# Turning w3 by DMA transposes, splitting the first turns and reordering the first loads in a fused attention and feed-forward kernel

## The chip, the cores and the metric

The kernel runs on one core of a Trainium2 chip. The metric is the device time of one execution in microseconds (us), the median of three runs. Engines are named as in the profile: PE is TensorE (its matrix multiplies), PEld its weight loads, DVE is VectorE, ACT is ScalarE, POOL is GpSimd and SP is SyncE. DMAs that POOL issues go by a software queue, which here also rounds float32 to bf16 on the way; those that SP issues go by a hardware queue.

## The reference, cut to what matters

Eight batches of eight heads, 576 positions, 64 features a head. Heads 0 to 3 attend to the last 32 positions; heads 4 to 7 to every fourth of the last 128. Heads are joined and go through a multiplicative feed-forward block with no nonlinearity behind the product, so that `w3 @ w_out` can be formed once and used in place of two products.

```python
scores = (1/8) * q @ k.T                       # per batch and head
rel = pos[:, None] - pos[None, :]
mask_plain = (rel >= 0) & (rel < 32)            # heads 0..3
mask_dil = (rel >= 0) & (rel < 128) & (rel % 4 == 0)   # heads 4..7
attn = softmax(where(mask, scores, -1e9)) @ v
x = attn.transpose(0, 2, 1, 3).reshape(4608, 512)
h = (x @ w1) * (x @ w2) @ w3                    # w1, w2: 512 x 1024; w3: 1024 x 1024
out = h @ w_out                                 # w_out: 1024 x 512
```

## The kernel before, in words

All products run on PE in bf16 with float32 sums in PSUM, which is one tile `ps` of eight banks. The work is cut into tasks. Python code adds each task to a `Plan` with a name, an engine, a duration in ns that is written in the code, the tasks that it depends on, a priority and the number of PSUM banks that it needs. `Plan.run` (lines 70 to 156) walks through time with these durations and gives the order of the tasks and the banks of each; the instructions are then issued in that order, and each engine works through its own part of it strictly in order. So a guess of the planner that is too short makes an engine stand at a wait with later work queued behind it. Loads are tasks of a queue called "DMA": POOL issues them one after the other, and it waits before each for the landing of the load eight places earlier.

What the tasks do:

- `Lqn`, `Lkn`, `Lvn` load q, k and v of one batch (lines 220 to 225), `LW` loads one half of the columns of w1 or w2, `LWO` half of w_out, `LW3.f` rows 128f to 128f+127 of w3. The first q and k (heads 0 to 3 of batch 0) come as float32 by SP into `gt` and are rounded by ACT (`Cqn`, `Ckn`, lines 229 to 240).
- `T...` are DVE block transposes of q, k and v into `qt`, `kt` and `vt` (lines 337 to 357). Heads 0 to 3 are called u = 0, heads 4 to 7 u = 1; for u = 1, and for q of u = 0 too, the four residues of the position modulo 4 are stored one after the other, 144 positions each. `VT` and `VK` bring v of the batches 0 and 1 back by PE transposes (line 366) and copies.
- `S` are scores of a group of blocks of 96 queries (line 408). In the batches 0 and 1 the mask comes as a bias that PE adds first (line 391), from a small table that POOL (`band`) and ACT (`blocks`, lines 308 to 319) make at the start. `E` is the exponential on ACT, `V` the product with v (line 444), `R` and `N` the division on DVE, `X` and `K` the turn back by PE (line 484) and a copy. From batch 2 on a DMA transpose on SP (`XD`, line 497) does the turn back.
- `A` and `B` are the products with w1 and w2 for one of 16 units k of 288 tokens and one of eight column blocks f (line 516, four matmuls each); ACT copies A (`CA`) and DVE multiplies (`G`, line 532).
- `W3T`, `W3C`, `W3M`, `W3D` form `w3 @ w_out`: per row block f of w3, eight PE transposes (line 573) into a PSUM bank, a copy to SBUF by ACT (line 580), eight matmuls (line 585) and a copy to `wf_sb` by DVE (line 595).
- `Y` is the product with `wf_sb` for 128 tokens (line 543); it needs all eight blocks of `wf_sb`. ACT copies it (line 554) and SP stores it.

The order of the first loads is: batch 0, w1 and w2 (two halves each), w_out (two halves), six blocks of w3, batch 1, the last two blocks of w3, then batch 2. The order of A and B is unit by unit, f from 0 to 7. Before unit 0, PE runs `WARM` = 12 matmuls on zeros.

Of the kernel before, what the change touches and what calls it, by code (L numbers as in the profile page):

```python
# [29 lines left out]
BIASED = 2  # L30
TURNED = 2
ORDER = (2, 3, 0, 1)
RANK = dict(E=1.5, VK=1, K=0.4, N=3, T=1.5, VT=0.2, S=0.3, V=0.1, X=0.4)
WARM = 12
W3_FIRST = 6
SHIFT = {}
ON_DVE = ("K0.0", "K0.2", "K0.3", "K1.2", "VK0.1.0", "VK1.0.1")
GRP = 5
WHOLE = ("qn", "kn")
TURN_LAT = 2700  # L40
LEAD = 1.4

# [12 lines left out]
class Plan:  # L55
# [14 lines left out]
    def run(self):  # L70
# [41 lines left out]
        while len(order) < n:  # L112
            progress = True
            while progress:
                progress = False
                for e in engines:
                    if free[e] > now:
                        continue
                    for r, t in sorted(waiting[e], key=lambda x: x[1].prio):
                        if r > now:  # L120
                            continue
                        at = place(t) if t.slot else 0
                        if at is not None:
                            break
                    else:
                        continue
                    waiting[e].remove((r, t))
                    t.start = now
                    if e == "DMA":
                        free[e] = now + t.dur[0]  # L130
                        dma = max(dma, now + t.dur[0]) + t.dur[1]
                        t.end = dma + 1900
                    else:
                        t.end = free[e] = now + t.dur
                        if t.lat == TURN_LAT and dma > now:
                            t.lat += 3300
                    if t.slot:
                        t.place = at
                        held[at : at + t.slot] = [t] * t.slot
                        if t.slot == 4:  # L140
                            kept = None
                    order.append(t)
                    for u in users[id(t)]:
                        left[id(u)] -= 1
                        if not left[id(u)]:
                            r = max(d.end + (0 if d.eng == u.eng else d.lat) for d in u.deps)
                            waiting[u.eng].append((r, u))
                    progress = True
# [11 lines left out]
def kernel(  # L160
# [27 lines left out]
    wk_pool = ctx.enter_context(tc.tile_pool(name="wk", bufs=2))  # L188
    w3_pool = ctx.enter_context(tc.tile_pool(name="w3", bufs=8))
    ps_pool = ctx.enter_context(tc.tile_pool(name="ps", bufs=1, space=bass.MemoryType.PSUM))  # L190
# [62 lines left out]
    def load_v_dil(b, m):  # L253
        vp = vps[b % 2]
        r, mu = 2 * (m // 3), m % 3
        runs = {
            0: [(0, 96, r, 0)],
            1: [(0, 48, r, 96), (48, 48, r + 1, 0)],
            2: [(0, 96, r + 1, 48)],
        }[mu]  # L260
# [9 lines left out]

    def load_w(dst, src, c):
        f = slice(512 * c, 512 * (c + 1))
        nc.gpsimd.dma_start(
# [34 lines left out]
    def blocks():  # L308
# [3 lines left out]
        base = bias[:, 6, :]  # L312
        by_res = base.rearrange("p (t r) -> p r t", r=4)
        nc.scalar.copy(
            out=bias[:, 0:4, :].rearrange("p i (r t) -> p i r t", r=4),
            in_=by_res.unsqueeze(1).to_broadcast([P, 4, 4, 24]),
        )
        nc.scalar.copy(out=bias[:, 4, :], in_=base)
# [18 lines left out]
    def turn(b, u, nm, part):  # L337

        src = qk[(nm, b)][:, u, :].bitcast(U32)
        dst, pad = {"qn": (qts, 0), "kn": (kts, PADK), "vn": (vts, PADK)}[nm]  # L340
        d = dst[b % len(dst)].rearrange("p u w c -> p u (w c)").bitcast(U32)[:, u, :]
        if part is None:
            o = d[:, pad : pad + S].rearrange("p (j a) -> p a j", a=18)
            nc.vector.transpose(out=o, in_=src.rearrange("p (a i) -> p a i", a=18))  # L344
            return
        n, first, odd = ((5, 0, 2 * RUN + 4), (4, 2 * RUN, 5 - 2 * RUN))[part]
        o = bass.AP(
            tensor=d.tensor,
            offset=d.offset + pad + first,
            ap=[d.ap[0], [1, n], [RUN, 2], [9, 16], [odd, 2]],  # L350
        )
        i = bass.AP(
            tensor=src.tensor,
            offset=src.offset + part * 64,
            ap=[src.ap[0], [128, n], [32, 2], [1, 32]],
        )
# [200 lines left out]
    def store(i):  # L557
# [3 lines left out]
        while at < end:  # L561
            n = min(end, (at // RUN + 1) * RUN) - at
            b, x = at // S, at % S
            row = b * S + 4 * (x % RUN) + x // RUN
            nc.sync.dma_start(
# [3 lines left out]

    def w3_back(ft):  # L570
        x = bank(KFF * P, BF16).rearrange("p (g x) -> p g x", g=KFF)
        for g in range(KFF):
            nc.tensor.transpose(  # L573
                out=x[:, g, :], in_=w3n[ft][:, g * P : (g + 1) * P], identity=ident
            )
        held[("x3", ft)] = x

    def w3_keep(ft):
        w3T[ft] = wk_pool.tile([P, KFF, P], BF16, tag="w3T", bufs=2, name="w3T")
        nc.scalar.copy(out=w3T[ft], in_=held[("x3", ft)])  # L580

# [11 lines left out]

    def w3_done(ft):
        nc.vector.tensor_copy(out=wf_sb[:, ft, :], in_=held[("wf", ft)])

# [45 lines left out]
    def loads_v(b):  # L642
# [5 lines left out]
        ]  # L648

    def loads_w12(c):  # L650
        return [
            load("LW", 800, 3300, [], lambda d=d, s=s: load_w(d, s, c))
            for d, s in ((w1_sb, moe_w1), (w2_sb, moe_w2))
        ]
# [7 lines left out]
    for u in range(2):  # L662
        for nm in ("qn", "kn", "vn"):
            if u or nm not in WHOLE:
                loads_rows(nm, 0, (u,))
    idt = add("ident", "DMA", (600, 0), [], lambda: make_identity(nc, ident), 2.5, lat=-1900)
    bnd = add("band", "DMA", (700, 0), [c0], band, 2.6, lat=-1800)
    blk = add("blocks", "ACT", 1200, [bnd], blocks, 0, lat=100)
    blk = add("no halo", "DVE", 150, [blk], no_halo, 0, lat=80)
    mk = add("masks", "DMA", (2500, 0), [blk], masks_of_bias, 26.5, lat=-1800)  # L670
    lw12 = [loads_w12(0), loads_w12(1)]
    for c in range(2):
        lwo[c] = load(f"LWO{c}", 600, 3300, [], lambda c=c: load_wo(c))
    def loads_w3(fts):
        for ft in fts:
            lw3[ft] = load(f"LW3.{ft}", 550, 1400, [], lambda ft=ft: load_w3(ft))

    loads_w3(range(W3_FIRST))
    for nm in ("qn", "kn", "vn"):
        loads_rows(nm, 1)  # L680
    loads_w3(range(W3_FIRST, KFF))

    FUSED, w3m = [], []
    for ft in range(KFF):
        x = add(f"W3T{ft}", "PE", 510, [lw3[ft], idt], lambda f=ft: w3_back(f), 6, slot=1,
                after=[w3m[-2] if len(w3m) > 1 else None])
        y = add("W3C", "ACT", 1012, [x], lambda f=ft: w3_keep(f), -1, lat=100,
                after=[w3m[-2] if len(w3m) > 1 else None])
        z = add(f"W3M{ft}", "PE", 1728, [y, lwo[0], lwo[1]], lambda f=ft: w3_mul(f), 7, slot=1)
        w3m.append(z)  # L690
        FUSED.append(add("W3D", "DVE", 688, [z], lambda f=ft: w3_done(f), -1, lat=100))

# [4 lines left out]
    def turns(b, u, nm, pr):  # L697
        parts = (None,) if u == 0 and nm != "qn" else (0, 1)
        old = last_v.get((b - 1, u)) if nm == "vn" else last_s.get((b - 2, u))
        ts = [  # L700
            add(f"T{nm}{b}.{u}.{part or 0}", "DVE",
                1245 if part is None else 750 if part == 0 else 630, [L[(nm, b, u)], c0],
                lambda part=part: turn(b, u, nm, part), pr, lat=80, after=[old])
            for part in parts
        ]
        turned.setdefault((nm, b), []).extend(ts)
        return ts

    vals, T = {}, {}
    for b in range(B):  # L710
# [4 lines left out]
        for u in range(2):  # L715
            T[(b, u)] = [
                t for nm in ("kn", "qn") for t in turns(b, u, nm, 10 * b + RANK["T"])
            ]
        for u in range(2):
            if b >= 2:  # L720
                break
            tv = turns(b, u, "vn", 10 * b + RANK["T"])
            for half in range(2):
                x = add(f"VT{b}.{u}.{half}", "PE", 420, tv + [idt],
                        lambda b=b, u=u, h=half: v_back(b, u, h), b - 99 + RANK["VT"], slot=1)
# [6 lines left out]
                ]  # L732
        if b >= 2:
            hal = add(f"HALO{b}", "DVE", 820, LV[b], lambda b=b: halo_v(b), 10 * b + 2, lat=80)
            for u in range(2):
# [4 lines left out]
        def group(blocks, biased):  # L740
# [3 lines left out]
            n = f"{b}.{2 * u + m // 3}.{m % 3}"  # L744
            need = [t for at in sorted({x[0:2] for x in blocks}) for t in T[at]]
            old = readers.pop(n_grp - len(ets), [])
# [69 lines left out]
    def ups(k, f):  # L816
        nonlocal seq
        b, hf = k // 2, k % 2
        need = kept[b][0:2] + kept[b][2 + hf : 3 + hf]
        wl = lw12[f // 4]  # L820
        lap = k * UNIT - RING
# [25 lines left out]
    done = 0  # L847
    for k in range(2 * B):
        for f in range(KFF):
            ups(k, f)  # L850
            if f % 3 == 1 and done < n_y and (done + 1) * P <= k * UNIT:
                downs(done)
                done += 1
    while done < n_y:
# [43 lines left out]
```

## Time and profile before

| | |
|---|---|
| median of three runs | 259.79 us (259.71 to 260.15) |
| the profiled execution | 260.15 us |
| its span, first to last instruction | 258.4 us |
| mean granted PE clock | 0.985 |
| busy: PE / DVE / ACT / POOL | 246.9 / 166.2 / 122.9 / 65.0 us |
| w3's transposes on PE (line 573) | 64 instructions |
| w3's copies on ACT (line 580) | 8 of 1012 ns |

The profiled execution is one of the three, the longest: its time is 1.75 us more than its span, and 0.36 us more than the median. In the profile, a busy time is the time in which an engine had an instruction in it; matmuls overlap, so that the time that one of them adds to a stream is less than its own duration. The chain of waits, which is followed back from the last instruction, shows what each one adds. A DMA's time runs from its issue to its landing.

### The profile page before, as it was taken

The page shows a single profiled execution, that of the slowest core. Times are in us where ns is not written, and L with a number is a line of the kernel's source. Part 1 is how long each engine was busy: PE and PEld are TensorE (multiplying, and loading weights), DVE is VectorE, ACT ScalarE, POOL GpSimd, SP SyncE. Part 2 cuts the span into 40 slices and gives each one's busy share as a digit, 9 for nine tenths or more (in the row PEclk, how much of TensorE's full clock was granted, in tenths as well). Part 3 has the DMA queues.
Part 4 walks back from the last instruction along what each step waited for, and adds up shares of the span by engine and source line. Part 5 has one row for each costly group of instructions (what it writes and reads, how often), then busy time and mean ns, then how long its engine had stood idle before and what let it go on. Part 6 is the DMA issues. An engine that isn't in the chain of part 4 may idle for free.

```text
span 258.4 us, 6741 instructions
## 1 busy us (share of the span) xinstructions
PE 246.9 (96%) x2732; PEld 168.1 (65%) x2732; DVE 166.2 (64%) x338; ACT 122.9 (48%) x211; POOL 65.0 (25%) x101
## 2 busy tenths in 40 slices
PE   6589999999999999999999999999999999999993
PEld 2367865576577676676667766677766766777661
DVE  3966436979898898898858687666654653333220
ACT  4465464493826373453653535636355343333331
POOL 8612476265401728232023050300000000000000
PEclk9689999999999999999999999999999999999999
DMA  7999999999999999999983949652417172211113
GB/s 224 204 206 200 210 213 210 201 90 193 153 177 159 182 186 128 163 184 213 213 89 49 106 56 143 101 75 55 91 39 93 41 91 63 83 39 43 43 41 122
DMA packets 58030, 33.40 MB, mean 129 GB/s; under 512 B 44688, under 2 KB 47760, under 8 KB 58000
## 3 DMA queue, kind: packets, MB, share of 16 engines
q0 software_dynamic: 37488, 18.81, 57.4%
q1 hardware_dynamic: 20512, 14.16, 26.8%
q8 instruction: 21, 0.34, 0.6%
q14 instruction: 9, 0.07, 0.1%
HBM read 38.80 MB, written 9.44 MB: 187 GB/s over the span
## 4 chain that ended last, share of the span: by engine, by line
PE 92%; ACT 2%; DVE 2%; DMA 2%; issue 0%; ACTq 0%; DVEq 0%
PE ps L516 49%; PE ps L543 24%; PE ps L585 5%; PE ps L444 5%; PE ps L408 4%; ACT et L419 2%; PE ps L391 2%; DMA gt<-in_q_dram 2%; PE ps L366 1%; PE ps L573 1%; PE ps L484 1%; DVE qt L357 1%; DVE kt L344 0%; ACT qn L240 0%; DVE vt L344 0%
## 5 line engine op out<-in xcount | busy, mean ns | idle before, releaser
L516 PE MATMUL ps<-XT,w_sb 128*128 128x288 bf16 x1024 | 136.0, 286 | 0.2 <-DVE gt L532 0.2
L516 PEld LDWEIGHTS <-w_sb 128*128 128x128 bf16 x1024 | 97.6, 98 | 30.2 <-issue 0.6
L532 DVE TENSOR_TENSOR gt<-ps,asb 128x288 bf16<-128x288 f32 x128 | 57.9, 454 | 55.2 <-PE ps L516 53.5
L527 ACT CAST asb<-ps 128x288 bf16<-128x288 f32 x128 | 50.9, 398 | 60.5 <-PE ps L516 57.7
L543 PE MATMUL ps<-wf_sb,gt 128*128 128x512 bf16 x288 | 67.7, 379 | 0.0
L554 ACT COPY osb<-ps 128x512 f32<-128x512 f32 x36 | 21.1, 585 | 52.5 <-PE ps L543 52.5
L543 PEld LDWEIGHTS <-gt 128*128 128x128 bf16 x288 | 28.0, 98 | 27.7
L262 POOL DMA_DIRECT2D vp<-in_v_dram x48 | 30.0, 631 | 49.2 <-PE ps L444 16.2
L419 ACT ACTIVATE et<-ps 128x1920 bf16<-128x1920 f32 (+2 forms) x23 | 34.4, 1506 | 5.9 <-PE ps L408 4.7
L467 DVE TENSOR_TENSOR xo<-ps,rcp 96x384 bf16<-96x384 f32 (+1 forms) x48 | 31.8, 678 | 0.6
L357 DVE STREAM_TRANSPOSE qt<-qn 128x320 uint32<-128x320 uint32 (+1 forms) x32 | 21.6, 675 | 3.3 <-ACT qn L240 3.1
L427 DVE TENSOR_TENSOR et<-et,mask 128x960 bf16<-128x960 bf16 (+1 forms) x30 | 18.1, 630 | 3.8 <-ACT et L419 3.6
L444 PEld LDWEIGHTS <-et 128*128 128x128 bf16 x384 | 14.5, 98 | 3.8 <-ACT et L419 1.3
L444 PE MATMUL ps<-vp,et 128*128 128x65 bf16 x384 | 15.6, 195 | 1.0 <-ACT et L419 1.0
L585 PE MATMUL ps<-wo_sb,w3T 128*128 128x512 bf16 x64 | 15.0, 379 | 0.0
L408 PEld LDWEIGHTS <-kt 32*128 32x128 bf16 x768 | 9.5, 95 | 6.1 <-issue 5.6
L357 DVE STREAM_TRANSPOSE kt<-kn 128x320 uint32<-128x320 uint32 (+1 forms) x16 | 10.9, 681 | 3.6 <-PE ps L408 3.5
L408 PE MATMUL ps<-qt,kt 32*128 32x96 bf16 x768 | 12.9, 206 | 0.0
L344 DVE STREAM_TRANSPOSE kt<-kn 128x576 uint32<-128x576 uint32 x8 | 10.0, 1249 | 2.0 <-PE ps L408 2.0
L580 ACT COPY w3T<-ps 128x1024 bf16<-128x1024 bf16 x8 | 8.1, 1012 | 4.8 <-PE ps L573 4.7
L455 DVE RECIPROCAL rcp<-ps 96x12 f32<-96x12 f32 x32 | 6.5, 214 | 5.6 <-PE ps L444 5.5
L248 POOL DMA_DIRECT2D vp<-in_v_dram x6 | 7.3, 1209 | 10.6 <-PE ps L444 10.6
(49 smaller groups left out, 105.4 us busy)
## 6 DMA issues: line engine op xcount, KB each, us to landing
qn<-in_q_dram POOLq DMA_DIRECT2D x7, 576.0 KB, 8.0
kn<-in_k_dram POOLq DMA_DIRECT2D x7, 576.0 KB, 9.0
w_sb<-in_moe_w_dram POOLq DMA_DIRECT2D x4, 512.0 KB, 12.3
w3n<-in_moe_w_dram POOLq DMA_DIRECT2D x8, 256.0 KB, 15.2
out_dram<-osb SPq DMA_DIRECT2D x8, 256.0 KB, 2.8
out_dram<-osb SPq DMA_DIRECT2D x8, 224.0 KB, 2.8
vp<-in_v_dram POOLq DMA_DIRECT2D x6, 288.0 KB, 10.3
out_dram<-osb SPq DMA_DIRECT2D x8, 192.0 KB, 2.6
```

What stands on the lines that cost most here:

```text
L262: nc.gpsimd.dma_start(out=vp[32 + p0 : 32 + p0 + n, 4:8, m, 0:D], in_=v_rows(b, 4, 4 * t0 + res, [[4 * D, n], [S * D, 4], [1, D]]),)
L357: nc.vector.transpose(out=o, in_=i)
L408: nc.tensor.matmul(out=self.sp[:, g, QB * i : QB * i + QB], lhsT=kt[prt, u, QB * m : QB * m + P, c], rhs=qq, start=(c == 0 and not biased) ...
L419: nc.scalar.activation(out=ev, in_=self.sp[:, :, 0:x], func=ACT.Exp, scale=scale)
L444: nc.tensor.matmul(out=self.o[:, g, mm, :], lhsT=grp.et[:, c0 : c0 + P], rhs=vps[self.b % 2][:, 4 * self.u + g, 3 * self.hf + mm, 0 : D + ...
L467: nc.vector.tensor_tensor(out=dst, in0=self.o[0:QB, hs, :, 0:D], in1=self.rcp[0:QB, hs, :].unsqueeze(3).to_broadcast([QB, n, 3, D]), op=AL ...
L516: nc.tensor.matmul(out=o, lhsT=w_sb[:, c, f * P : (f + 1) * P], rhs=unit_cols(k, c), start=(j == 0), stop=(j == DCH - 1),)
L527: nc.scalar.copy(out=a_sb, in_=held[("a", k, f)])
L532: nc.vector.tensor_tensor(out=gt[:, f, c0 : c0 + UNIT].rearrange("p (r m t) -> p m r t", r=2, m=BLK), in0=held[("b", k, f)].rearrange("p ( ...
L543: nc.tensor.matmul(out=y, lhsT=gt[:, f, c0 : c0 + P], rhs=wf_sb[:, f, :], start=(f == 0), stop=(f == KFF - 1),)
L554: nc.scalar.copy(out=o_sb, in_=held[("y", i)])
L585: nc.tensor.matmul(out=o, lhsT=w3T[ft][:, g, :], rhs=wo_sb[:, g, :], start=(g == 0), stop=(g == KFF - 1),)
```

## The change

Five things change, and the planner lays out all tasks anew.

1. w3 is turned by DMA transposes. `W3T` and `W3C` go; a task `XW` on SP (`w3_turn`) reads one block `w3n` of 128 x 1024 bf16 in SBUF and writes it turned to `w3T`. There are three buffers of `w3T` in place of two, so that XW of block f waits for the matmuls `W3M` of block f-3; and seven of `w3n` in place of eight, so that the load of block 7 waits for XW of block 0. Of the copies `W3D`, five go from DVE to ACT.
2. In batch 0 the turns of q, k and v of heads 4 to 7 are cut into two halves by residue. The residues are stored in the order 0, 2, 1, 3, so that the even tokens can be turned, and their scores begun, first.
3. The first loads come in another order: w1 and w2 in pieces of 256, 256 and 512 columns with block 0 of w3 between them, then batch 1, block 1 of w3, w_out, and blocks 2 to 7 of w3, of which block 7 comes in the midst of batch 2's loads.
4. The units 0 and 1 are interleaved: f = 0 to 3 of both, then f = 4 to 7 of both.
5. `blocks` gets a priority that puts it ahead of `Cqn` and `Ckn` on ACT; its widest copy becomes two; `WARM` is 16; other priorities, the list of copies that go to DVE, and the planner's durations of DMAs are new.

```diff
-RANK = dict(E=1.5, VK=1, K=0.4, N=3, T=1.5, VT=0.2, S=0.3, V=0.1, X=0.4)
-WARM = 12
-W3_FIRST = 6
+RES = (0, 2, 1, 3)
+RANK = dict(E=2, VK=2, K=1.5, N=0.3, T=0.5, VT=0.4, S=0.1, V=0.2, X=0.4)
+WARM = 16
+FIRST_LOADS = ("w0", "30", "w1", "w2", "q1", "k1", "v1", "31", "o0", "o1", "32", "33", "34", "35", "36", "37")
...
-ON_DVE = ("K0.0", "K0.2", "K0.3", "K1.2", "VK0.1.0", "VK1.0.1")
+ON_DVE = ("K0.1", "K0.2", "K0.3", "K1.2", "VK1.0.0", "VK1.1.0", "VK1.1.1", "W3D2", "W3D3", "W3D4")
...
+BUSY_LAT = 3300
...
-                        if t.lat == TURN_LAT and dma > now:
-                            t.lat += 3300
+                        if e == "SP" and t.lat >= TURN_LAT and t.name[0] == "X" and dma > now:
+                            t.lat += BUSY_LAT
+                            dma += t.lat / 6
...
-    w3_pool = ctx.enter_context(tc.tile_pool(name="w3", bufs=8))
+    w3_pool = ctx.enter_context(tc.tile_pool(name="w3", bufs=7))
...
-        n, first, odd = ((5, 0, 2 * RUN + 4), (4, 2 * RUN, 5 - 2 * RUN))[part]
+        n, first, odd = ((5, 0, RUN + 4), (4, RUN, 5 - RUN))[part % 2]
+        low = max(0, part // 2 - 1)
+        both = 2 if part < 2 else 1
...
-    def w3_back(ft):
-        x = bank(KFF * P, BF16).rearrange("p (g x) -> p g x", g=KFF)
-        for g in range(KFF):
-            nc.tensor.transpose(
-                out=x[:, g, :], in_=w3n[ft][:, g * P : (g + 1) * P], identity=ident
-            )
-        held[("x3", ft)] = x
-
-    def w3_keep(ft):
-        w3T[ft] = wk_pool.tile([P, KFF, P], BF16, tag="w3T", bufs=2, name="w3T")
-        nc.scalar.copy(out=w3T[ft], in_=held[("x3", ft)])
+    def w3_turn(ft):
+        w3T[ft] = wk_pool.tile([P, KFF, P], BF16, tag="w3T", bufs=3, name="w3T")
+        nc.sync.dma_start_transpose(out=w3T[ft], in_=w3n[ft])
...
-    blk = add("blocks", "ACT", 1200, [bnd], blocks, 0, lat=100)
+    blk = add("blocks", "ACT", 1200, [bnd], blocks, -5, lat=100)
...
+    WC = (slice(0, 256), slice(256, 512), slice(512, 1024))
...
-    for ft in range(KFF):
-        x = add(f"W3T{ft}", "PE", 510, [lw3[ft], idt], lambda f=ft: w3_back(f), 6, slot=1,
-                after=[w3m[-2] if len(w3m) > 1 else None])
-        y = add("W3C", "ACT", 1012, [x], lambda f=ft: w3_keep(f), -1, lat=100,
-                after=[w3m[-2] if len(w3m) > 1 else None])
-        z = add(f"W3M{ft}", "PE", 1728, [y, lwo[0], lwo[1]], lambda f=ft: w3_mul(f), 7, slot=1)
+    for ft in sorted(lw3):
+        x = add(f"XW{ft}", "SP", 100, [lw3[ft]], lambda f=ft: w3_turn(f), -1, lat=3600,
+                after=[w3m[-3] if len(w3m) > 2 else None])
+        if ft + 7 in lw3:
+            lw3[ft + 7].after.append(x)
+            lw3[ft + 7].deps.append(x)
+        z = add(f"W3M{ft}", "PE", 1728, [x, lwo[0], lwo[1]], lambda f=ft: w3_mul(f), 7, slot=1)
...
-            parts = (None,) if u == 0 and nm != "qn" else (0, 1)
+            parts = (2, 3, 4, 5) if b == 0 else (0, 1)
...
+    half = KFF // 2
+    begin = [(k, f + h) for h in (0, half) for k in range(2) for f in range(half)]
+    for k, f in begin + [(k, f) for k in range(2, 2 * B) for f in range(KFF)]:
```

In the new order on PE, the matmuls of blocks 0 and 1 of w3 stand after the first `V` of batch 1, those of the blocks 2, 3 and 4 one after the other in the midst of unit 2, block 5 after the first scores of batch 2, block 6 after the next ones, and block 7 in unit 3. On SP, the eight XW stand right behind the two first loads and ahead of all other transposes and stores.

## The prediction

> **What bounds the kernel now.** I read the page first: who is busy, when, and who makes the chain that ended last.
>
> ```profile
> PE 246.9 (96%) x2732; PEld 168.1 (65%) x2732; DVE 166.2 (64%) x338; ACT 122.9 (48%) x211; POOL 65.0 (25%) x101
> ...
> PE   6589999999999999999999999999999999999993
> ...
> DMA  7999999999999999999983949652417172211113
> ...
> PE 92%; ACT 2%; DVE 2%; DMA 2%; issue 0%; ACTq 0%; DVEq 0%
> ```
>
> PE is the bound from the fourth slice on (a slice is 6.46 us): whatever leaves PE there shortens the run, if nothing else is late. The DMA row has nines over the first 19 slices, some 120 us: the loads run without a pause. Next the chain in order of time, where w3 is made into w3 @ w_out:
>
> ```profile
> 33.84 0.45 PE ps L573 x8
> 34.29 0.98 PE ps L516 x8
> 35.27 0.45 PE ps L573 x8
> 35.72 1.73 PE ps L585 x8
> ```
>
> PE goes from one task to the next with no gap; eight transposes of w3 (L573) add 0.45 us, eight matmuls with w_out (L585) 1.73, four of L516 0.49. PE's own waits:
>
> ```profile
> PE ps L366 <- DVE vt L344: 4.0, 1, 4.0
> PE ps L604 <- DVE warm L607: 1.2, 1, 1.2
> PE ps L444 <- ACT et L419: 1.0, 2, 0.8
> ```
>
> Past the 4.0 us ahead of v's first turn PE waits some 2 us in all. The start, by windows (PE busy first, the clock third from the end):
>
> ```profile
> 8.00:10.00 2.00, 0.34 (x4) 0.34 (x5) 2.00 (x3) 0.00 (x0) 1.45 (x2) 0.54 1.10 207
> 10.00:12.00 2.00, 2.00 (x15) 1.37 (x13) 1.97 (x6) 1.48 (x2) 0.54 (x2) 0.50 1.15 199
> ...
> 16.00:18.00 2.00, 1.24 (x43) 0.82 (x41) 1.97 (x4) 1.76 (x2) 0.53 (x1) 1.00 1.25 211
> ```
>
> The clock is at half from about 8.2 to 15 us. Last, issue to landing: the loads of w3 (L288), then the transposes of attention's output (L497) while loads run (73 to 119 us), then without loads (from 150 us):
>
> ```profile
> DMA to landing us min/median/max: 12.5/15.2/18.3
> ```
>
> ```profile
> DMA to landing us min/median/max: 5.2/7.5/8.3
> ```
>
> ```profile
> DMA to landing us min/median/max: 2.6/3.4/5.2
> ```
>
> The transposes that the change adds run beside the loads, so the middle row prices them.
>
> **The sum** starts from the profiled execution, 260.15 us (span 258.4); it lies 0.36 above the median of 259.79, which I take off at the end. The tail after PE's last matmul is untouched.
>
> **PE transposes of w3 go.** 8 times 0.45 us, all on the chain: -3.6. ACT loses eight copies of 1012 ns and gets five of 585, DVE loses five of 692; between 34 and 48 us both are busy about half the time, so that counts nothing.
>
> **The start: +0.5.** Before, ACT rounded q from 4.73 and k from 6.08 (1.15 us each), and `blocks` came after. Now `blocks` stands ahead of both and waits for POOL's band, which ends at 4.49. Its copies took 0.54 + 0.27 + 0.23; with the widest in two pieces of some 0.36, 1.2. So q is rounded from 5.8, k until 8.1; DVE turns q (1.41) until 8.4, k (1.24) until 9.6. The first scores start at 9.65, where PE stood at v's turn (9.66) before. From there, at half clock: two groups of scores, 1.56 and 1.67, v's turns 1.46, until 14.3; exponentials (1.13) and v copies (0.80) in ACT's new order end at 16.85 (third exponential), 17.65 and 19.0. On DVE eight half turns (about 0.5 of 0.73 and 0.62 each) last until 15, then the divisions of 0.95 and the copies; the one that unit 0 needs ends at 21.7. Before, unit 0 began at 21.2. Bounds: at full clock the two groups and the turns save 2.2, ACT's chain then ends 1.3 earlier, so -0.8; with every half turn at the whole one's price, +1.0. Four more warm-up matmuls at 0.22 lie in the 4.0 us wait and cost nothing; without that cover 0.9.
>
> The last warm-up matmul ended at 5.69 and the clock fell at about 8.2, 2.5 us later; now it ends near 6.6, and the scores at 9.65 come 3.0 us later, so I take the low clock. The Trainium skill (TensorE: Matmul & The Clock Gate, "What's actually happening") lets the clock fall only after an idle window of some 3.4 us: by that rule it would stay up, and the time would be about 1.3 us less.
>
> **The waits for turned blocks: +1.2.** When does PE need them? Unit 0 from 21.7; 32 tasks of 0.49 and one X of 0.26 bring it to 37.7; the scores and turns of batch 1 took 5.85 (48.84 to 54.69); three V and short waits, 1.5. Block 0 at 45.1 to 46.8, block 1 at 47.1 to 48.8. Then two X, a V, six tasks of 0.49, an X, and 0.5 of waits, 4.6: block 2 at 53.4, 3 at 55.1, 4 at 56.8 to 58.6. Six tasks, scores of 0.55, a task: block 5 at 62.6; 6 at 64.9.
>
> When do they come? The landings move with the order. The first rows end at 11.7; w1 and w2 take 10.7, a w3 block 1.25, batch 1's q, k, v 8.8, w_out 5.3. Block 1 lands at 33.6 and block 2 at 40 to 41. A transpose takes 7.5 us by the row beside loads, but a block of w3 has 262 KB where attention's has 147, 1.78 times. Three of attention's landed 0.6 us apart when the loads had ended (81.3, 81.9, 82.4) and 2.4 apart beside them (109.1, 111.3, 113.9): +0.5 or +1.9. I take 8.2, nearer the first, since most of the 7.5 is waiting and not transfer. Bounds: 3.4 (no load beside it) and 13.4 (all of 7.5 grows by 1.78). Blocks 1 and 2 come at 42 and 49, in time. Then three buffers bind: block 3's transpose starts when block 0's matmuls end, 46.8, and lands at 55.0 (needed 55.1); block 4's at 57.0 (56.8); block 5's at 63.3; block 6's at 65. With each wait moving what follows: 0.2 + 0.5 = 0.7. If instead one must be through before the next (4.3 apart, 1.78 times 2.4), block 4 waits 2.5 and block 6 0.5: 3.0. The three at 109 to 114 had 8.2 each and did not add up, so nearer the first: 1.2. By the outer bounds: 0, or 10.4 (5.1 at block 3, 0.3, 0.5, 4.5).
>
> Who stands behind: on PE everything; on DVE the copies of blocks 2 to 4 are ahead of the turns of batch 2, whose scores come after block 5 anyway; on SP only the next transposes (the first XD is issued past 70 us); on POOL the last loads of batch 2 stand behind block 7's load, which waits for block 0's transpose, issued at 16, and so for nothing.
>
> **The rest: +0.3.** Batch 1's scores and the begin of unit 2 wait for ACT and DVE some 0.3 more than the 0.7 before, since less PE work is interleaved with them. The order of f, the residues' order and the loads' pieces leave counts and durations as they are: 0 (w's pieces of 256 columns are ready at 18, needed from 21.7; that cover gone, 1.3 each).
>
> Sum: -3.6 + 0.5 + 1.2 + 0.3 = -1.6; 260.15 - 1.6 - 0.36 = **258.2**. Own range: waits of 0 and a start of -0.8 give 255.7, waits of 2.2 give 259.2.
>
> **Rival 1, slower: transposes land in the order of issue.** The POOL row "14.55 ... [2.01 <-DMA w_sb" says that eight loads are always queued, 12 to 18 us deep. All ten transposes from 73 to 119 us landed between 1.2 before and 1.5 after the last load issued ahead of them (100.8 to 109.06: the load ahead landed at 109.77). If that holds at depth, with 1.4 us of DMA time each: block 1 (issued at 35.0 behind seven loads) lands at 48.0, block 2 behind q and k of batch 2 at 55.1, block 3 behind v at 58.9, block 6 behind batch 3 at 70.9. Waits: 0.9, 0.7, 2.1, 0.1, 2.2: 6.0. The time is 260.15 - 3.6 + 0.5 + 0.3 + 6.0 - 0.36 = **263.0**. It decides from waits of 2.8, a latency near 9.5 us. Against it: none of the ten had more than 9.1 us of loads ahead.
>
> The Trainium skill (DMA: Bandwidth & Descriptors, "Queues, rings and completion order") says that a DMA engine takes the queues that have work in turn, a packet of one at a time. By that rule a transpose waits for one load's packet and not for seven loads, and the forecast stands; by the landings above alone it would be the rival.
>
> **Rival 2: no change.** The transposes come in time, but each adds its packets to a full DMA, eight times 1.0 to 1.4 us, and batch 2 and the transposes of blocks 4 to 6 slip: waits near 2.8, within 0.5 of 259.8.
>
> **How the numbers follow.** Forecast 0.50, rival 1 0.33, rival 2 0.17, of which I give 0.10 to a change within 0.2% (0.5 us, about what a measurement of this kernel can tell from none) and 0.07 to slower. So faster 0.50, same 0.10, slower 0.40. The range, 255.9 to 263.4, takes in the own range but for its foot, rival 2, and rival 1 with 0.4 to spare; outside it lie rival 1 with still longer waits (up to the 10.4 above, 267.4) and little else.
>
> **What would show it.** In the profile after: no PE transposes of w3; transposes `w3T<-w3n` on SP with 7 to 9 us to landing (right), 12 or more (rival 1); PE's waits at the matmuls with w_out near 1 us or near 6; the clock still at half until about 15 us and unit 0 at 21.7. A first XD or store held up, or scores of batch 2 waiting for q, would make the sum wrong in a way not foreseen.

## The result, and the profile after

The changed kernel takes 277.31 us (four runs, 274.29 to 278.63) where the kernel before took 259.97 beside it. The ratio is 1.063, with a 95% interval of 1.054 to 1.071. It is slower by 6%, and the forecast of 258.2 us was wrong, as was its range. The profiled execution of the changed kernel took 274.29 us, with a span of 272.5 us. (The kernels in which DMA turns w3 scatter by up to 4% from one execution to the next, and a few executions of the others are longer too; a ratio is made from undisturbed executions alone.)

The page of the changed kernel, the lines that answer to those shown of before:

```profile
PE 247.4 (91%) x2672; PEld 165.2 (61%) x2672; DVE 164.7 (60%) x340; ACT 115.7 (42%) x208; POOL 66.2 (24%) x103
...
PE   8679896099599997999999999999999999999993
...
PEclk9999999569979999999999999999999999999998
DMA  7999999999999499979989953972232232212113
...
PE 70%; DMA 24%; POOL 2%; ACT 1%; issue 1%; DVE 0%; SPq 0%; DVEq 0%; POOLq 0%; ACTq 0%
```

PE is no busier than before (247.4 to 246.9 us: 3.6 us of transposes went, and work at half clock came), but it has holes: the eighth slice (47.7 to 54.5 us) is a zero. In and behind the holes its clock is down. DMA is 24% of the chain where it was 2%. PE's waits, in total us, number and longest:

```profile
PE ps L587 <- DMA w3T<-w3n: 12.2, 3, 8.6
PE ps L418 <- DVE kt L352: 2.1, 1, 2.1
PE ps L454 <- DVE vp L276: 1.4, 1, 1.4
```

L587 are the matmuls with w_out, and they wait for turned blocks: 12.2 us where the sum had 1.2. The chain from 36 to 79 us (start, us, what):

```profile
36.67 17.15 DMA w3T<-w3n
...
53.87 3.60 PE ps L587 x8
...
64.09 11.20 DMA w3T<-w3n
...
75.34 3.14 PE ps L587 x8
```

Block 1's transpose took 17.15 us from issue to landing, and PE stood for 8.60 of them; block 5's took 11.20, and PE stood for 3.19. The packet records divide block 1's time: 3.8 us from the issue to its first packet, 12.3 for its 1024 packets of 256 bytes (40.48 to 52.74 us), 1.1 from the last one to the landing. The transposes go through their queue one after another: block 2 was issued at 43.46, but its first packet follows block 1's last, at 52.76. Eight matmuls that take 1.73 us at full clock take 3.60 and 3.14 right after. The line of the transposes in the code (L582), issue to landing:

```profile
DMA to landing us min/median/max: 8.6/11.4/17.1
```

By stretches (us, PE busy first, the granted clock third from the end):

```profile
6.00:8.00 2.00, 0.75 (x6) 0.29 (x3) 1.70 (x3) 1.39 (x2) 1.84 (x4) 1.00 1.09 200
8.00:10.00 2.00, 1.14 (x44) 0.79 (x48) 2.00 (x3) 0.65 (x1) 1.29 (x2) 1.00 1.10 207
...
43.00:54.00 11.00, 2.40 (x25) 1.30 (x22) 3.62 (x7) 1.13 (x2) 6.60 (x9) 0.75 1.13 190
54.00:59.00 5.00, 5.00 (x33) 2.74 (x32) 0.46 (x1) 1.13 (x2) 1.15 (x2) 0.52 1.59 145
```

At the start the clock stays at full speed, against the forecast. PE's order of time there (start, us, what, and the wait ahead of it):

```profile
6.10 0.65 PE L401 MATMUL ps<-bias,ident 128*128 128x288 bf16 x4
8.86 0.44 PE L418 MATMUL ps<-qt,kt 32*128 32x96 bf16 x24 [2.10 <-DVE kt L352]
```

The bias matmuls of the first group need only the mask blocks, which are ready early now; they run right behind the warm-up, and PE then stands 2.1 us and not 3. Unit 0 begins at 18.83 us where it began at 21.17.

So the span grew by 14.1 us in this way: turns -3.6, start -2.3, waits for turned blocks +12.2, and PE's work at half clock +4.2 (4.9 us of it from 53.87 to 58.77 and 3.4 from 75.84 to 79.25, half of which is extra). Some 3.6 remain, 2.2 of which are new waits for gt (0.8) and v (1.4); the last 1.4 were not taken apart.

### The profile page after: what moved, and what is told of

It is laid out like the page before. It is cut to its first block, busy times and chain, and to the rows that moved or that the text cites. A ratio compares the mean times of both kernels' runs of the same rounds, so it can differ in the third digit from the quotient of the medians.

```text
span 272.5 us, 6621 instructions
## 1 busy us (share of the span) xinstructions
PE 247.4 (91%) x2672; PEld 165.2 (61%) x2672; DVE 164.7 (60%) x340; ACT 115.7 (42%) x208; POOL 66.2 (24%) x103
## 4 chain that ended last, share of the span: by engine, by line
PE 70%; DMA 24%; POOL 2%; ACT 1%; issue 1%; DVE 0%; SPq 0%; DVEq 0%; POOLq 0%; ACTq 0%
PE ps L526 39%; PE ps L553 20%; DMA w3n<-in_moe_w_dram 11%; DMA w3T<-w3n 10%; PE ps L587 4%; PE ps L454 3%; DMA out_dram<-osb 3%; PE ps L418 3%; ACT et L429 1%; ACT osb L564 1%; POOL w_sb L279 1%; PE ps L494 0%; POOL vn L232 0%; DVE vp L276 0%; POOL qn L232 0%
## 5 line engine op out<-in xcount | busy, mean ns | idle before, releaser
L269 POOL DMA_DIRECT2D vp<-in_v_dram x48 | 29.8, 626 | 57.5 <-PE ps L454 21.2
L587 PE MATMUL ps<-wo_sb,w3T 128*128 128x512 bf16 x64 | 17.9, 434 | 12.2 <-DMA w3T<-w3n 12.2
L367 DVE STREAM_TRANSPOSE qt<-qn 128x320 uint32<-128x320 uint32 (+3 forms) x34 | 22.5, 665 | 2.8 <-DMA qn<-in_q_dram 1.6
L587 PEld LDWEIGHTS <-w3T 128*128 128x128 bf16 x64 | 6.4, 106 | 20.8 <-DMA w3T<-w3n 13.1
L367 DVE STREAM_TRANSPOSE kt<-kn 128x320 uint32<-128x320 uint32 (+3 forms) x18 | 11.6, 645 | 0.6 <-PE ps L418 0.4
L598 ACT CAST wf_sb<-ps 128x512 bf16<-128x512 f32 x5 | 2.9, 585 | 21.0 <-PE ps L587 20.9
L232 POOL DMA_DIRECT2D kn<-in_k_dram x8 | 5.5, 690 | 21.3 <-DVE kt L367 18.8
```

The costliest lines, as they stand in the source:

```text
L269: nc.gpsimd.dma_start(out=vp[32 + p0 : 32 + p0 + n, 4:8, m, 0:D], in_=v_rows(b, 4, 4 * t0 + res, [[4 * D, n], [S * D, 4], [1, D]]),)
L367: nc.vector.transpose(out=o, in_=i)
L587: nc.tensor.matmul(out=o, lhsT=w3T[ft][:, g, :], rhs=wo_sb[:, g, :], start=(g == 0), stop=(g == KFF - 1),)
```

## The experiments

Theory A is the prediction's rival 1: a transpose lands after the loads that were issued ahead of it, so that the depth of the queue makes it late. Theory B: the DMA engines take one packet of the transpose and one of a load in turn, so that each of its 1024 packets waits for a load's packet, whatever stands behind that. Theory C: it is other parts of the change that cost.

**All but the turns (e1).** The task `XW` is taken out, and PE's transposes and ACT's copy are put back; the planner lays the tasks out anew.

```diff
-        x = add(f"XW{ft}", "SP", 100, [lw3[ft]], lambda f=ft: w3_turn(f), -1, lat=3600, ...
+        t = add(f"W3T{ft}", "PE", 510, [lw3[ft], idt], lambda f=ft: w3_back(f), 6, slot=1, ...
+        x = add("W3C", "ACT", 1012, [t], lambda f=ft: w3_keep(f), -1, lat=100, ...
```

> Everything of the change but one part: w3 is turned on PE and copied by ACT again, as in the kernel before. If the turned blocks are what costs (theories A and B alike, whatever makes them late), the 12.2 us of waits at the matmuls with w_out and the some 4.4 us of PE work at half clock that follow them go, the eight PE turns (3.6 us) come back, and the earlier start (unit 0 at 18.8 instead of 21.2 us) stays: 255.5 to 258.5 us, below the kernel before. If other parts cost (theory C: the load order, the halves of batch 0, the rounding), it stays above 262 us.

Measured: 257.11 us (median of 257.09 to 268.71; ratio to before 0.988, 0.986 to 0.990). Unit 0 begins at 18.88 us, the clock is full until the last 1.3 us, and the chain reads

```profile
PE 88%; DVE 5%; ACT 3%; issue 2%; POOL 1%; POOLq 0%; DVEq 0%; ACTq 0%
```

Theory C falls. The DMA turns, with the order that the planner makes for them, account for the 20.2 us between the medians of the two kernels, and the rest of the change is worth 3.2 us (before took 260.31 beside it).

**The turns alone, in the old order (e4).** The kernel before, with `XW` in place of `W3T` and `W3C`, three buffers of w3T and seven of w3n.

> The kernel before with one part of the change alone: w3 turned by DMA transposes (three buffers), in the old load order, where the blocks of w3 land at 29 to 35 us ahead of batch 1 and are needed early. Theory A (order of issue): the transposes are issued right behind the landings, and each lands when the loads queued at its issue have landed, by 46 us for the first six: PE loses some 3 to 8 us, 261 to 266 us. Theory B (packets in turn): each transpose takes some 12 us of its own beside loads of 2 KB packets, the three that are in flight one after another: block 0 lands near 44, the next ones 5 to 12 us apart, and PE loses 10 us or more: above 270 us.

Measured: 277.64 us (ratio 1.068, 1.064 to 1.072), as slow as the whole change. The first six turned blocks land at 46.7, 55.1, 58.6, 62.1, 63.0 and 65.2 us. PE at the matmuls with w_out:

```profile
46.79 0.61 PE L577 MATMUL ps<-wo_sb,w3T 128*128 128x512 bf16 x1 [9.50 <-DMA w3T<-w3n]
...
55.18 5.47 PE L577 MATMUL ps<-wo_sb,w3T 128*128 128x512 bf16 x16 [4.80 <-DMA w3T<-w3n]
```

Theory A had all six landed by 46 us; the first was, nearly, and the others came 8 to 18 us later, the last ones close together, beside v's small packets. (Blocks 3 to 5 were issued only from 51.4 us on, since three buffers bind; blocks 0 and 1 were issued at 29.23 and 30.62.) The landings themselves speak against theory A: block 1 landed 8.9 us after the last of the loads issued ahead of it (46.28), behind block 0 in the transposes' own queue, while in the changed kernel block 0 landed at 31.28 us, 4.1 ahead of the last of the seven loads issued before it (35.38). Neither the new load order nor the order on PE is needed for the loss.

**A shallow queue (e2).** The changed kernel; each load on POOL's queue also waits for the landing of the load three places earlier (eight before).

```diff
+DEPTH = 3
...
+        if len(queue) >= DEPTH:
+            tc.add_manual_dep(
+                i.ins,
+                queue[-DEPTH].ins.name,
...
```

> The changed kernel with the same order of work, but each load on POOL's queue is issued only when the load three places ahead of it has landed, so that at most three are queued where there were eight to eleven. Theory A (a transpose lands after the loads issued ahead of it, so the depth of the queue makes it late): block 1's transpose takes 7 to 9.5 us in place of 17.2, PE's waits for turned blocks fall from 12.2 to below 3 us, and the time to 262 to 267 us. Theory B (each of a transpose's 1024 packets takes turns with a load's packet of some 2 KB, however many loads are queued): block 1's transpose still takes 12 us or more, the waits stay above 7 us, and the time is 271 to 279 us.

Measured: 289.08 us (287.0 to 297.2), ratio 1.108 (1.101 to 1.116). Its transposes, issue to landing, and the wait for them:

```profile
DMA to landing us min/median/max: 4.1/13.7/19.2
```

```profile
PE ps L588 <- DMA w3T<-w3n: 13.0, 3, 7.3
```

The landing of block 1 itself is not in the records, but its last packet is, 13.0 us after the issue, where theory A had the landing at 7 to 9.5; the next five landed after 10.9, 17.3, 19.2, 16.5 and 6.5 us, with at most three loads queued. A queue of less than half the depth does not make the transposes early. But the packets of e2 were themselves slow in long stretches (from 64 to 66 us 61 packets of each queue a us, where 91 go in the changed kernel), so that it gives no price. Theory A falls by the packets of the changed kernel too: block 1's begin 3.8 us after the issue and go among those of the seven loads issued ahead of it, the last of which landed at 50.71 us. The kernel became slower than both theories said; PE waits 3.9 us for w1 and w2 there, which it did not before, and the rest was not taken apart. The packets of the two queues between 64 and 66 us (q0 is POOL's queue, q1 SP's; packets, MB, share of the engines' time):

```profile
q0 software_dynamic: 124, 0.28, 108.7%
q1 hardware_dynamic: 122, 0.03, 42.4%
```

One for one, as in the changed kernel, from 46 to 52 us beside loads with packets of 2 and 2.3 KB:

```profile
q0 software_dynamic: 546, 1.10, 95.7%
q1 hardware_dynamic: 547, 0.14, 17.0%
```

and from 56 to 58 us, beside v's packets of 128 bytes:

```profile
q1 hardware_dynamic: 747, 0.18, 81.5%
q0 software_dynamic: 750, 0.10, 77.5%
```

These rows give the price, by the rate. (The times of the packets cannot simply be added: the shares of the two queues sum to more than 100%, so packets overlap.) In the first stretch of the changed kernel 547 transposed packets went in 6 us, 91 a us, so that a block of 1024 takes 11.2 us; block 1 took 12.3, since from 44 to 46 us the packets of both queues went at half the rate (105 of each in 2 us). With 3.8 us ahead and 1.1 behind, that is its 17.15. Beside v's packets 374 go a us, and a block takes 2.7 (block 3's packets went from 57.35 to 60.40).

**Smaller packets in the loads (e5).** The changed kernel, with each block of w3 loaded in packets of 512 bytes.

```diff
-        nc.gpsimd.dma_start(out=w3n[ft], in_=moe_w3[ft * P : (ft + 1) * P, :])
+        rows = moe_w3[ft * P : (ft + 1) * P, :].rearrange("p (b a x) -> p a b x", a=2, b=2)
+        for a in range(2):
+            nc.gpsimd.dma_start(
+                out=w3n[ft][:, 512 * a : 512 * a + 512].rearrange("p (b x) -> p b x", b=2),
+                in_=rows[:, a, :, :],
+            )
...
-                lhsT=w3T[ft][:, g, :],
+                lhsT=w3T[ft][:, (0, 1, 4, 5, 2, 3, 6, 7)[g], :],
```

> The changed kernel, but each block of w3 is loaded in two pieces whose rows are not contiguous in memory, so that it comes in packets of 512 bytes in place of 2048 (the columns are permuted, and the matmuls with w_out take w3T's groups in the permuted order); bytes, order and transposes are the same. Theory B (one packet of the transpose for one packet of a load): beside the blocks a transposed packet waits for a quarter of the bytes, so block 1's transpose falls from 17.2 us to 8 to 11, the wait for it from 8.6 to below 3 us, and the time to 264 to 271 us; the rate in the packet records goes from some 95 transposed packets per us to over 200 there. A rival, B2 (a transpose is slow by its own work or by the bytes that share the engines, whatever their packets): still some 17 us, 8 us of wait, and 274 to 279 us.

Measured: block 1's transpose took 10.6 us in place of 17.15, and PE's wait for it was 2.28 us in place of 8.60. From 42 to 45 us, beside w3's loads, the packets went

```profile
q0 software_dynamic: 738, 0.36, 88.2%
q1 hardware_dynamic: 725, 0.19, 46.8%
```

Nearly one for one again, 242 transposed packets per us where 91 went beside 2 KB: 4.2 us a block at that rate. Block 1's packets took 5.7 us in all (41.94 to 47.64, a slow last us included) where they took 12.3. Block 0, whose neighbours are the same loads as before, took 15.73 us from issue to landing where it took 15.40. The one other thing that the edit changes is that a block's load is two DMAs, so that the queue's places hold fewer bytes; but block 1's packets begin 3.9 us after the issue, as in the changed kernel, and it is their rate beside the loads that rose. This is theory B, and B2 falls; a transpose is not slow by its own work either, for the last block of e2, with little beside it, needed 1.6 us for its 1024 packets. The time did not follow: 274.98 us (269.24 to 278.19), too wide a scatter for a ratio. The profile is of an execution of 273.75 us; in it the gain at block 1 went again at the blocks 2 and 3, which took 13.0 and 17.0 us (block 3's first packet came 8.5 us after its issue, behind block 2's last):

```profile
48.68 1.90 PE L592 MATMUL ps<-wo_sb,w3T 128*128 128x512 bf16 x8 [2.28 <-DMA w3T<-w3n]
...
58.51 3.40 PE L592 MATMUL ps<-wo_sb,w3T 128*128 128x512 bf16 x8 [3.51 <-DMA w3T<-w3n]
65.89 6.54 PE L592 MATMUL ps<-wo_sb,w3T 128*128 128x512 bf16 x16 [3.98 <-DMA w3T<-w3n]
```

From 53 to 56 us all packets of both queues were slow:

```profile
DMA packets 226, 0.19 MB, mean 63 GB/s; under 512 B 76, under 2 KB 174, under 8 KB 226
```

That is 63 GB/s with every DMA engine busy, where 182 went from 42 to 45 us. The packet records show such stretches in the kernels with PE's turns too, but mostly of one or two us. What makes them, and what the kernel of e5 would take without them, is open.

**Is the half clock a cost of its own? (e3)** The changed kernel, with matmuls on zeros in the two long waits.

```diff
+        for _ in range({1: 36, 5: 14}.get(ft, 0)):
+            nc.tensor.matmul(out=o, lhsT=warm[:, 0:P], rhs=warm, start=True, stop=True)
```

> The changed kernel with matmuls on zeros in the two long waits (36 of 128x512 ahead of block 1's matmuls, 14 ahead of block 5's), so that PE does not stand idle there; nothing else is changed. If the half clock after the waits (48.5 to 58.8 and 75.8 to 79.3 us) is a cost of its own, it goes, and the time falls by 2.5 to 4.4 us, to 271 to 274. If the half clock only lies where PE waits again anyway, the waits grow by as much as the clock gives back, and the time stays at 275 to 278.

Measured: 279.24 us (278.68 to 281.52), ratio 1.075 (1.069 to 1.081). The clock did stay up behind block 1 (clock third from the end):

```profile
54.00:59.00 5.00, 4.77 (x53) 3.40 (x55) 2.15 (x5) 1.91 (x5) 1.16 (x2) 1.00 1.79 102
```

and PE was through with block 2 at 61.98 us, where the changed kernel only began it at 62.17. But then it stood 1.9 us ahead of block 3, which landed at 63.84, and 4.0 ahead of block 4:

```profile
63.89 1.90 PE L589 MATMUL ps<-wo_sb,w3T 128*128 128x512 bf16 x8 [1.91 <-DVE qt L367]
69.81 3.60 PE L589 MATMUL ps<-wo_sb,w3T 128*128 128x512 bf16 x8 [4.02 <-DMA w3T<-w3n]
```

(The first of these is put down to DVE, but block 3's transpose landed 0.05 us before the matmuls began.) So the 4.2 us at half clock are hardly a cost of their own here: the rate at which turned blocks arrive sets the pace from 45 to 75 us, and a faster PE waits for the next block instead. The fillers ahead of block 5 ran for 3.2 us from 78.21, when PE had work (block 5's last packet had gone at 69.81), which is why it is rather slower; without them the time would be near 276 us, an estimate from the two, and still not the 271 to 274 of a cost of its own.

**Was the order only laid out for too short a latency? (e6)** One number of the changed kernel's planner.

```diff
-        x = add(f"XW{ft}", "SP", 100, [lw3[ft]], lambda f=ft: w3_turn(f), -1, lat=3600,
+        x = add(f"XW{ft}", "SP", 100, [lw3[ft]], lambda f=ft: w3_turn(f), -1, lat=10000,
```

> The changed kernel with one number changed: the planner that lays out the order of work is told 10.0 us for a turned block (13.3 beside loads) in place of 3.6 (6.9). Nothing on the chip gets faster; the matmuls with w_out move back and units come forward. If the loss is that PE's order asks for the blocks too early, the waits for turned blocks fall from 12.2 to below 4 us and the time to 259 to 265 us. If there is no other work to put in their place (gt's ring is full, the scores of batch 2 are not ready), the waits turn up elsewhere and the time stays above 270 us.

Measured: 275.12 us (271.09 to 277.32), ratio 1.048 (1.043 to 1.053), where the changed kernel had 1.063 (1.054 to 1.071). The waits, longest first:

```profile
PE ps L454 <- ACT osb L564: 5.0, 1, 5.0
PE ps L587 <- DMA w3T<-w3n: 4.9, 2, 4.4
```

The waits for turned blocks fell from 12.2 to 4.9 us, and a wait of 5.0 came at 100 us: six `Y` now follow one another, and their output buffers wait for stores that take 11.7 us among the loads. The planner's guess is a part of it at most. Put off, the blocks hold back `Y`, and the work comes late there.

**Three blocks by DMA, five by PE (e8).** From the kernel of e1.

```diff
+BY_DMA = (5, 6, 7)
+XW_LAT = 10000
```

> The kernel with PE turns (257.1 us), but blocks 5, 6 and 7 are turned by DMA, with the planner told 10.0 us (13.3 beside loads) for each, so that their matmuls come at about 67 to 75 us. Three times 0.45 us leave PE: 255.6 to 256.6 us if the blocks land by then. If they land later than that (17 us each and one after another), PE waits 1 to 5 us and the gain is gone: 257 to 261 us.

Measured: 262.01 us (twelve runs, 259.07 to 269.79), ratio 1.003 (1.001 to 1.005). The turned blocks were in time (they landed at 57.1, 59.0 and 67.9 us, and PE never waited for one). The loss is at the output buffers again, four `Y` close together and a store of 8.44 us; the clock is at half behind that wait, from 82.93 to 89.76 us, which costs up to another 3:

```profile
PE ps L528 <- ACT osb L566: 3.1, 1, 3.1
```

**Two blocks by DMA, four output buffers (e11).** From e8, with the buffers of w3T cut to two.

```diff
-BY_DMA = (5, 6, 7)
+BY_DMA = (6, 7)
...
-        o_sb = wk_pool.tile([P, d_model], F32, tag="osb", bufs=3, name="osb")
+        o_sb = wk_pool.tile([P, d_model], F32, tag="osb", bufs=4, name="osb")
...
```

> The kernel with PE turns (257.1 us), with blocks 6 and 7 alone turned by DMA (the planner told 10.0 us, 13.3 beside loads, so that their matmuls come near 72 us), and with four buffers for the output rows in place of three (two for w3T in place of three), since in the kernel with three blocks by DMA PE's longest wait (3.1 us) was for an output buffer whose store took 8.4 us beside the loads. If that wait was what ate the gain there, the time is 255.8 to 256.8 us. If the stores, or the loads of batches 2 and 3, are late by more because of the transposes' packets, it is 257.5 to 262 us.

Measured: 256.91 us (256.43 to 257.10), ratio 0.987 (0.985 to 0.989). The wait at the output buffers is gone. One of the two transposes took 4.5 us and the other 13.7, which the planner had allowed for. Against e1's ratio of 0.988 (0.986 to 0.990) no gain can be told apart: 0.9 us of PE work saved was expected and 0.2 came. Both versions are some 1.2% faster than the kernel before.

**The start (e7, e9, e10).** From e1. In e7 the mask blocks got their old priority.

> The kernel with the change's other parts and PE turns (257.1 us), but the mask blocks again come after q and k have been rounded, as in the kernel before: the bias matmuls of the first groups then cannot run in the gap behind the warm-up. If it is these matmuls that keep the clock up, the clock falls to half again from about 8 or 9 us until 14 to 15, unit 0 begins 1.5 to 2.5 us later than the 18.8 us it had, and the time is 258.5 to 260 us. If the 16 warm-up matmuls alone keep it up, the clock stays and the time is 256.8 to 257.6.

Measured: 257.10 us; but ACT's order was the same as in e1, because the band is ready before q has come and the planner takes what is ready. The edit moved nothing, and the run says only that 257.1 repeats. In e9 the blocks depend on the two roundings, as on ACT before, and e10 also has 12 warm-up matmuls:

```diff
-    blk = add("blocks", "ACT", 1200, [bnd], blocks, -5, lat=100)
+    blk = add("blocks", "ACT", 1200, [bnd, L[("qn", 0, 0)], L[("kn", 0, 0)]], blocks, -5, lat=100)
...
-WARM = 16
+WARM = 12
```

> The kernel with PE turns (257.1 us), but the mask blocks are made to wait until q and k have been rounded, as in the kernel before; the 16 warm-up matmuls stay. They end at 6.5 us, and the first bias matmuls then cannot run before about 8.4 us. If PE may stand idle some 2.5 us before the clock falls (before: 5.69 to 8.17), the clock stays up and the time is 257.2 to 258.0 us. If the bias matmuls at 6.1 to 7.1 us are what keeps the clock up, it falls to half near 9 us, unit 0 begins at 20.5 us or later in place of 18.9, and the time is 258.7 to 260.5.

> As the run with the mask blocks behind the rounding, but with 12 warm-up matmuls in place of 16, so that PE falls idle at 5.6 us and stands 2.8 us or longer. If the clock falls after some 2.5 us without work, it is at half from about 8.2 to 15 us as in the kernel before, unit 0 begins at 20.5 to 21.2 us, and the time is 258.7 to 260 us: the start's gain of the change would be the clock's. If the clock stays up, the gain is that of the earlier rounding and the half turns, and the time is 257.2 to 258.0 us.

Measured: e9 257.75 us (ratio 0.991, 0.989 to 0.992), e10 259.04 us (0.995, 0.993 to 0.996). PE's first bias matmuls, of e9 and then of e10:

```profile
8.96 0.65 PE L401 MATMUL ps<-bias,ident 128*128 128x288 bf16 x4 [1.29 <-DVE bias L329]
```

```profile
8.85 1.12 PE L401 MATMUL ps<-bias,ident 128*128 128x288 bf16 x4 [2.84 <-DVE bias L329]
```

They come at the same time, but in e10 PE had stood 2.84 us, and they run at half clock (0.70 from 8 to 10 us, 0.50 from 10 to 12); unit 0 begins at 19.59 us in e9 and 20.81 in e10. Part of e9's shorter gap is chance: in its profiled execution the clock rose at 7.02 us (5.39 in e10), so that the warm-up itself ran longer at half clock, until 7.67. But all four executions of e9 have a mean granted clock of 0.998 or more, and the five of e10 have 0.990 to 0.993. So of the 3.2 us that the rest of the change gains, 0.6 are the early mask blocks and 1.3 the four warm-up matmuls, by the clock. The last 1.2 (from before's 260.25 to e10) was not taken apart.

## Why the prediction was wrong, point by point

**The latency of a turned block is the term that failed.** The prediction took 8.2 us, from a row of 7.5 for attention's transposes "beside loads", and put the bounds at 3.4 and 13.4. Measured: 8.6 to 17.15. Its argument was "most of the 7.5 is waiting and not transfer", and it scaled the row by bytes. Of the row itself the argument holds: in the packet records of the kernel before, those ten transposes needed 3.8 to 5.8 us to their first packet and 0.6 to 3.0 for their 576. But block 1 needed 12.3 us for 1024 packets, since the transfer goes by the packets beside it, 91 a us beside 2 KB. The row came from elsewhere: from 73 to 119 us those transposes' packets ran beside v's packets of 128 bytes, or when few load packets were left. Between 104 and 107 us in the kernel before:

```profile
q0 software_dynamic: 2236, 0.29, 150.1%
q1 hardware_dynamic: 607, 0.22, 46.6%
```

Here it was not even one for one. The blocks of w3 are turned among 2 KB packets, and I did not look at what kind of load stood beside the row's transposes. Block 1 was also loaded 3 us later than reckoned (36.65 and not 33.6). With the landing at 53.8 in place of 42 and PE there at 45.3, the wait of 8.6 us follows.

**The overlap of the transposes** was wrong as well, but cost little. Transposes in flight together were reckoned at 8.2 us each from their own issue, and "one must be through before the next" was weighed and mostly set aside. The runs show the second: block 2's packets begin when block 1's end, and the blocks 1, 2 and 3 land at 53.82, 58.46 and 61.10 us. PE's long waits were for the blocks 1 and 5, whose packets stood behind no other transpose.

**Rival 1 had the sign, not the reason.** Its waits of 6.0 us were half of the 12.2, and the packets and landings above rule out its mechanism. The mark that I set, "12 or more (rival 1)", could not tell it from theory B; only the depth of the queue and the size of the packets could. Rival 2's waits of 2.8 were passed fourfold.

**The rule from the Trainium skill held beside these loads, and its use was wrong.** DMA: Bandwidth & Descriptors, "Queues, rings and completion order", says that an engine takes its queues in turn, a packet of each; here 547 packets went to 546 (though 607 to 2236 in the row above). The prediction concluded that a transpose "waits for one load's packet and not for seven loads". It waits for one load's packet with every packet of its own, 64 times on each of 16 engines if the 1024 are spread evenly. The count of the packets and the rate of the loads' packets in the kernel before (229 of w3's from 28 to 30 us) would have said so: 1024 turns at 115 a us are 9 us of transfer at the least.

**PE's transposes** went as reckoned, -3.6.

**The start** was put at +0.5 and was -2.3. The forecast had the first scores at 9.65 and PE idle for 3.0 us until then; they came at 8.86, since `blocks` ran from 4.24 to 5.18 and q was rounded from 5.08 (5.8 in the sum); and the bias matmuls, which need no q and no k, fill part of the gap from 6.10. Against e1, e9 shows that the clock can stay up without that, and e10 that it falls without the four more warm-up matmuls, which the forecast counted as worth nothing. The sum's own bound at full clock, -0.8, was passed by 1.5 us, which was not taken apart further. The rule of TensorE: Matmul & The Clock Gate ("What's actually happening"), weighed there, has the clock fall after an idle window of 3.4 us. The clock stayed up here, but e10 shows it fall after a gap of 2.84, as before did after 2.5: 3.4 us is no safe bound on a gap.

**The order around it** held: the copies, turns and loads that were said to be hidden cost nothing visible in e1. What the sum had no term for is that late blocks pull the first `Y` together, so that the stores' latency among loads (7.3 us at 97 us in the changed kernel, 11.7 in e6) comes onto PE's path.

## What to carry to other kernels

A DMA transpose that shares its engines with loads is priced by its packets and the rate at which the load beside it gives up turns (91 a us beside 2 KB here, 242 beside 512 bytes, 374 beside 128), so look up which load that is, and take a row for such a transpose only where the same kind of load ran. Work that PE does in 0.45 us was dear on the DMA engines, which were off the chain in the profile before but full where the work was to stand. When a stream of inputs sets the pace, a faster clock or a better order for the engine behind it may only move the wait, as in e3 and e6.

## What the runs showed of the hardware that was not expected

Two DMA queues that both had work mostly got the same number of packets and not the same bytes: 547 to 546 beside 2 KB, 725 to 738 beside 512 bytes, 747 to 750 beside 128 bytes. The queue with 256-byte packets got a ninth to two thirds of the bytes accordingly. It is no law: beside 128-byte packets the loads also got 2236 to 607 in the kernel before (104 to 107 us), and when the loads' queue was shallow the transposes got more (1051 to 643 in e2, 46 to 55 us). What decides was not found.

DMA transposes in one queue went strictly one after another: block 2's first packet came 0.02 us after block 1's last, 9.3 us after its own issue.

In these traces PE's granted clock changes only on a grid of some 3.41 us, which lies differently in each execution: it was at half from 8.16 to 14.99 us in the kernel before (6.83), and from 48.53 to 58.77 and 75.84 to 79.25 in the changed one (10.24 and 3.41). The grid window in which the clock was lost in the kernel before, from 4.75 to 8.16 us, had PE at work in its first 0.94 us, so such a window need not be idle throughout.
